# Two layers of memory attention and FFN on one core: the first tiles one by one, two pairs of heads by column tiles, other times in the planner

## The chip, the cores and the metric

The kernel runs on one core of a Trainium2 chip. The metric is the device time of one execution in microseconds (us), lower is better; before the change the median of three runs is 567.0 us (565.68 to 568.76). Engines: PE (TensorE, matmuls; PEld are its weight loads), ACT (ScalarE), DVE (VectorE), POOL (GpSimd) and SP (SyncE), which issues nearly all DMA transfers from one queue, in order.

## The reference

Two layers over x of 2048 tokens by 640 features, in bf16. Each layer is an attention with a compressive memory, then an FFN, both on a layer norm without weights, both added to x:

```python
x = x + _A_ref(_layernorm(x), A_wq, A_wk, A_wv, A_wo, A_beta)
x = x + _B_ref(_layernorm(x), B_w1, B_w2)
x = x + _A_ref(_layernorm(x), A_wq, A_wk, A_wv, A_wo, A_beta)
x = x + _B_ref(_layernorm(x), B_w1, B_w2)
```

The attention has 32 heads of 20 features and cuts the tokens into 4 segments of 512:

```python
for s in range(N):                                  # N = 4
    logits = einsum('bhqd,bhkd->bhqk', qs, ks) * scale + mask
    a_dot = einsum('bhqk,bhkd->bhqd', softmax(logits), vs)
    pq = phi(qs)                                    # x+1 above 0, exp(x) else
    a_mem = (pq @ M) / (pq @ z + 1e-6)
    outs.append(g * a_mem + (1 - g) * a_dot)        # g = sigmoid(beta)
    M, z = M + phi(ks)^T @ vs, z + sum(phi(ks))
o = concat(outs) @ wo
```

The FFN is `relu(x @ w1) @ w2` with 1728 hidden features.

## The kernel before

The kernel is a program that plans itself. Each part of the work is a Python generator (a stream) that yields operations with an assumed duration, what they wait for, and the buffers (`Slot`) that they need. `Sched.run` takes again and again the operation that can start first by its own clock, ties by the stream's priority, and so writes a fixed instruction order for every engine; semaphore waits come only from data and buffers. `late` plays a finished order again with random delays of the transfers, and the best of 32 plans, which differ in the assumed price of a mode change on PE, is emitted. Wrong assumed times make no wrong result; they make an order in which an engine stands waiting in front of work that is ready behind it.

`Sched.keep_busy` (L627 in the profile) puts dummy matmuls on PE where the order has a gap of PE over 0.3 us. `ld`, `late_loads` and `turn` hold the assumed times of loads and of DMA transposes (`lat` is the time from the last byte to the semaphore, `holds` says that the queue stays taken). All the DMA transposes, loads, spills and fills go through SP's queue.

The stages. A tile is 128 tokens, a segment four tiles, a chunk 128 of the 640 features.

- The head: `first_ln_a` normalises tiles 0 and 1 with statistics on DVE (`stats`, L651), `first_ln_b` tiles 2 and 3, tile 2 with two ACT passes that sum (L753, L757), tile 3 on DVE. `chain` (L665) raises the variance to -1/2 on POOL, `normed` (L705) writes the normalised tile, and `first_pair` transposes it on PE (L728) into one of the four `MISC` banks of PSUM and copies it to xnT (L734 on DVE, L735 on ACT). `proj_first` then projects segment 0 to q and k, in groups of five matmuls over 256 tokens each (`group`, L640 and L643; copies to `stg` at L816, L817). When both halves of a chunk's q and k are there, `first_heads` (L913) sends the first heads to `pad`. `consts` begins its POOL memsets (L580 to L594) when all four tiles are transposed. `phi_` (L956, L963, L964) makes phi of q and k, `spill` (L889) and `fill` (L934) bring the other heads through DRAM.
- Attention: groups of four heads, eight groups a segment, two groups a pair (`m`, 32 pairs in both layers). `scores` (L1103) runs row-tiled matmuls into X and Y, two slots of two PSUM banks; `exps` (L1155) takes the exponentials on ACT; `causal` (L1167) masks on POOL; `apply` multiplies by the values.
- Values have two forms. Segment 0 of layer 0, pairs 0 to 3, goes through `values_by_token` (L1197): 40 matmuls a group, tokens on the partitions, and DVE divides straight out of PSUM (L1209, L1210, L1213). All other pairs use column tiles (L1246): 16 matmuls a group, four heads beside each other, heads on the partitions. The result is copied to `av` (L1254 on DVE, L1255 on ACT), transposed by a DMA to `avt` (`turn_av`) and divided there (`divide`, L1282, L1283, L1290). There is one `av` and one `avt`.
- `combine` adds what was read from the memory, `turn_o` transposes o_sb to oT by DMA, `out_proj` multiplies by wo and adds to x (L1317), `ln_b` normalises, `ffn` and `ffn_last` (L1394) follow. PE holds one of three tiling modes (full, rows, cols), and a change of it costs time, so the planner joins a column group to the rows in front of it where it can.

DMA transposes are recorded at L671, late loads at L528 to L536.

Of the kernel before, what the change touches and what calls it, by code (L numbers as in the profile page):

```python
# [6 lines left out]
dt = mybir.dt  # L7
ACT = mybir.ActivationFunctionType
ALU = mybir.AluOpType

T = 2048
D = 640
# [148 lines left out]
STARTS = [SWITCH_NS + 0.75 * (k - 32 // 2) for k in range(32)]  # L161
# [4 lines left out]
IDLE_NS = 300.0  # L166
COLD_NS = 8000.0
# [5 lines left out]
class Sched:  # L173
# [93 lines left out]
    def run(self):  # L267
        while True:
# [22 lines left out]
            for prio, n, st, alts, op, late in heads:  # L291
# [61 lines left out]
    def late(self, seed):  # L353
# [5 lines left out]
        for e, hold, tail, waits, out, is_dma in self.log:  # L359
            m = SEM_NS + (PE_MARGIN if e == "pe" else 0.0)  # L360
            start = max([t[id(k[0]), k[1]] + m for k in waits], default=0.0)
            start = max(free[e], start)
            free[e] = start + hold
            if is_dma:
                dma_free = max(dma_free, start + 300.0) + tail[1]
                land = max(dma_free, free[e]) + tail[0] + rnd.expovariate(1.0 / LATE_NS)
                if tail[2]:
                    free[e] = max(free[e], dma_free)
# [39 lines left out]
def plan(switch, sb, sem_, psum, dram, A_x, A_wq, A_wk, A_wv, A_wo, A_beta, B_x, B_w1, B_w2, out):  # L408
# [115 lines left out]
    def late_loads():  # L524
# [27 lines left out]
        for n, (name, nbytes, fn) in enumerate(pieces):  # L552
# [7 lines left out]
            tk = yield dma("sp", sems[name], nbytes, fn, w[:1] + (w2w if n >= n2 else []) + z1, issue=400.0, lat=4500.0)  # L560
# [96 lines left out]
    def chain(t0, n, tk, sq=None):  # L657
# [7 lines left out]
        tk = yield pool(760, lambda e: e.tensor_tensor(rstd[:, sl], lnU[:, sl], mhalf[:, 0:n], ALU.pow), [tk] + h)  # L665
        return tk

    def turn(slot_sem, dst, src, waits):
# [3 lines left out]
                       issue=max(1400.0, 140.0 * n), lat=2000.0, rate=270.0, holds=True)  # L672
        return tk

    def lnorm(s, x_tks, pool_, parts=1):
# [3 lines left out]
        for p0 in range(0, 4, n):  # L679
# [11 lines left out]
            for i in range(p0, p0 + n, 2):  # L691
# [6 lines left out]
                tT = yield from turn(xn_sem[id(bx)], xt.ap[:, i * FC:(i + 2) * FC, :], bx.ap, [t0, t1] + xt.tks)  # L698
# [10 lines left out]
    def first_pair(p, tch):  # L709
        idt = yield Need("ident")  # L710
        if p == 0:
            xt = yield Acq(XNT_A)
            xt.users = []
            S.set("xts", 0, 0, tks=[xt])
        else:
            xt = yield Need("xts", 0, 0)
            xt = xt[0]
        bx = yield Acq(XN)
        done = []
        tns = []  # L720
        for k in range(2):
            tn = yield normed(2 * p + k, k, bx, tch[k])
            tns.append(tn)
        for k in range(2):
            t = 2 * p + k
            tn = tns[k]
            pb = lambda bk: bk.ap.bitcast(dt.bfloat16)
            fns = [(lambda e, bk, c=c, k=k: e.transpose(  # L728
                pb(bk)[:, c * 128:(c + 1) * 128], bx.ap[:, k * D + c * 128:k * D + c * 128 + 128], ident[:]),
                c == FC - 1) for c in range(FC)]  # L730
            bk, tT = yield pe((88.0 if p == 0 else 56.0) * FC, fns, [tn] + idt, acq=MISC)
            dst = xt.ap[:, t * FC:(t + 1) * FC, :].rearrange("p c n -> p (c n)")
            src = pb(bk)[:, 0:D]
            tc = yield evac(D, 1.5, lambda e, dst=dst, src=src: e.tensor_copy(dst, src),  # L734
                            lambda e, dst=dst, src=src: e.activation(dst, src, ACT.Copy), [tT])  # L735
            bk.release(tc)
            done.append(tc)
        bx.release(tT)
        S.set("xt", 0, 0, p, tks=done)

    def first_ln_a():
        tch = []
        for t in range(2):
            w = yield Need(("x0a", "x0b")[t])
            tk = yield from stats(t, w)
            tk = yield from chain(t, 1, [tk])
            tch.append(tk)
        yield from first_pair(0, tch)

    def first_ln_b():  # L750
        w = yield Need("x01")
        junk = hT[:, 10:13, :].rearrange("p c n -> p (c n)")[:, 0:D]
        t0 = yield act(D + 350, lambda e: e.activation(  # L753
            junk, x_sb[:, 2, :], ACT.Copy, accum_out=asum[:, 0:1]), w, psum=False)
        tm = yield dve(2, 1, lambda e: e.tensor_scalar(
            mv[:, 2, 0:1], asum[:, 0:1], 1.0 / D, None, ALU.mult), [t0])
        t1 = yield act(D + 470, lambda e: e.activation(  # L757
            junk, x_sb[:, 2, :], ACT.Square, scale=-1.0, bias=mv[:, 2, 0:1],
            accum_out=asum[:, 2:3]), [tm], psum=False)
        t3 = yield from stats(3, w)  # L760
        t1 = yield dve(1, 1, lambda e: e.tensor_scalar(
            lnU[:, 2:3], asum[:, 2:3], 1.0 / D, LN_EPS, ALU.mult, ALU.add), [t1])
        t3 = yield dve(1, 1, lambda e: e.tensor_scalar(lnU[:, 3:4], mv[:, 3, 1:2], LN_EPS, None, ALU.add), [t3])
        h = yield Need("mhalf")
        tch = yield pool(760, lambda e: e.tensor_tensor(
            rstd[:, 2:4], lnU[:, 2:4], mhalf[:, 0:2], ALU.pow), [t1, t3] + h)
        yield from first_pair(1, [tch, tch])
# [56 lines left out]

    def proj_first():
# [740 lines left out]
```

## Time and profile before

| what | value |
|---|---|
| median of three runs | 567.0 us (565.68 to 568.76) |
| the profiled execution | 565.3 us, its span 563.5 us |
| granted TensorE clock | 1.00 |
| PE, DVE, ACT, POOL busy | 99%, 75%, 72%, 35% |
| chain that ended last | PE 87%, DVE 8%, DMA 2% |

The time of an execution is the span, from the first to the last instruction, and about 1.8 us around it. Rows of a timeline give the start, the duration, the engine (SPq is SP's queue), the line, the operation, output<-input, shapes and how many of them were merged; what stands in brackets is how long the engine had been idle and what released it. Rows of the waits give who waited for what: in total, how many times, and the longest. Matmuls are pipelined: the time that one takes from the engine is read from one start to the next, not from its duration.

### The profile page before, as it was taken

To read this page: it belongs to the slowest core of one execution; us is meant where nothing else is said; L and a number is where in the kernel's file an instruction comes from. 1 tells how busy PE (TensorE), PEld (TensorE's weight loads), DVE (VectorE), ACT (ScalarE), POOL (GpSimd) and SP (SyncE) were. 2 spreads that over 40 slices of the span, in tenths; PEclk is the share of its full clock that TensorE was granted. 3 is DMA by queue.
4 is the path that set the end of the run, shared out by engine and by line. 5 is a ranking of instruction groups with operands and counts; after the bars stand their busy time and mean duration, and the time that the engine had idled before them with its cause. 6 is when DMAs were issued, how large, how long until landed. Compare 5 with 4: busy or idle time off the path is not lost.

```text
span 563.5 us, 12875 instructions
## 1 busy us (share of the span) xinstructions
PE 556.4 (99%) x5219; PEld 305.0 (54%) x5219; DVE 420.1 (75%) x1070; ACT 404.2 (72%) x512; POOL 195.1 (35%) x302
## 2 busy tenths in 40 slices
PE   8999999999999999999999999999999999999998
PEld 7664555445554454645446544555445654665655
DVE  6989789888999689878898997688747964560202
ACT  4789998987788878778986688778878678113140
POOL 4544344333344335444433443035322433110000
PEclk9999999999999999999999999999999999999999
DMA  8695988383474136542375131880326410512101
GB/s 268 120 221 138 238 218 182 74 224 56 97 171 94 44 88 159 118 95 72 92 163 115 27 66 26 193 148 20 67 80 173 109 43 20 116 45 48 47 1 47
DMA packets 130109, 60.93 MB, mean 108 GB/s; under 512 B 108930, under 2 KB 119938, under 8 KB 130050
## 3 DMA queue, kind: packets, MB, share of 16 engines
q1 hardware_dynamic: 129830, 59.85, 45.5%
q8 instruction: 41, 0.67, 0.5%
q10 hardware_dynamic: 220, 0.26, 0.2%
q14 instruction: 18, 0.15, 0.1%
HBM read 20.57 MB, written 12.85 MB: 59 GB/s over the span
## 4 chain that ended last, share of the span: by engine, by line
PE 87%; DVE 8%; DMA 2%; ACT 1%; SPq 1%; issue 0%
PE ps L643 56%; PE ps L640 11%; PE ps L1103 8%; PE ps L1246 6%; DVE stats L651 2%; PE ps L996 2%; PE ps L1197 1%; PE ps L1047 1%; DVE x_sb L1317 1%; PE ps L1394 1%; DMA avt<-av 1%; DVE xn_tok L705 1%; SPq L913 1%; DMA oT<-o_sb 1%; ACT PT L1155 1%; DVE stg L816 1%
## 5 line engine op out<-in xcount | busy, mean ns | idle before, releaser
L1155 ACT ACTIVATE PT<-ps 128x1024 bf16<-128x1024 f32 x320 | 310.0, 1022 | 70.3 <-PE ps L1103 64.6
L1167 POOL TENSOR_SCALAR_AFFINE_SELECT PT<-PT 128x512 bf16<-128x512 bf16 x256 | 166.6, 668 | 268.2 <-ACT PT L1155 267.9
L643 PE MATMUL ps<-w_r,hT 128*128 128x320 bf16 (+2 forms) x768 | 123.0, 299 | 0.0
L643 PE MATMUL ps<-xnT,w_r 128*128 128x512 bf16 x416 | 113.3, 379 | 0.0
L1317 DVE TENSOR_TENSOR x_sb<-x_sb,ps 128x320 bf16<-128x320 bf16 (+1 forms) x128 | 60.3, 479 | 66.7 <-PE ps L643 66.0
L643 PEld LDWEIGHTS ps<-w_r,hT 128*128 128x128 bf16 x768 | 72.4, 98 | 31.9 <-issue 4.4
L1425 ACT ACTIVATE hT<-ps 128x512 bf16<-128x512 f32 x55 | 32.7, 598 | 50.0 <-PE ps L643 49.7
L1103 PE MATMUL ps<-pad 20*128 20x128 bf16 (+3 forms) x1024 | 64.8, 301 | 1.6 <-ACT PT L1155 0.9
L643 PEld LDWEIGHTS ps<-xnT,w_r 128*128 128x128 bf16 x416 | 39.7, 98 | 44.0 <-issue 3.2
L651 DVE BATCH_NORM_STATS2 stats<-x_sb 128x6 f32<-128x320 bf16 x126 | 56.4, 472 | 2.1 <-DMA x_sb<-in_A_x_dram 1.8
L1254 DVE CAST av<-ps 128x512 bf16<-128x512 f32 x53 | 36.2, 684 | 14.8 <-PE ps L1246 14.7
L1103 PEld LDWEIGHTS ps<-pad 20*128 20x128 bf16 x1024 | 18.3, 92 | 52.6 <-ACT PT L1155 25.6
L643 PE MATMUL ps<-wo_r,oT 128*128 128x320 bf16 x256 | 46.1, 299 | 0.0
L1246 PE MATMUL ps<-PT,v_aug 128*32 128x256 bf16 (+5 forms) x896 | 40.7, 302 | 0.0
L1423 DVE TENSOR_SCALAR hT<-ps 128x512 bf16<-128x512 f32 x49 | 33.4, 683 | 9.1 <-PE ps L643 9.0
L640 PE MATMUL ps<-xnT,w_r 128*128 128x512 bf16 x104 | 39.6, 380 | 0.0
L643 PE MATMUL ps<-wv_r,xnT 128*128 128x320 bf16 x192 | 36.7, 300 | 0.0
L643 PE MATMUL ps<-xnT,wk_r 128*128 128x512 bf16 (+1 forms) x140 | 36.1, 349 | 0.0
L643 PE MATMUL ps<-xnT,wq_r 128*128 128x512 bf16 (+1 forms) x140 | 34.9, 349 | 0.0
L665 POOL TENSOR_TENSOR rstd<-lnU,mhalf 128x2 f32<-128x2 f32 (+2 forms) x25 | 20.8, 831 | 38.0 <-DVE lnU L661 34.4
L816 DVE CAST stg<-ps 128x512 bf16<-128x512 f32 (+1 forms) x48 | 29.5, 618 | 3.3 <-PE ps L643 3.2
L1290 DVE TENSOR_TENSOR o_sb<-avt,rden 128x320 bf16<-128x320 bf16 x56 | 30.5, 562 | 0.6
(117 smaller groups left out, 695.8 us busy)
## 6 DMA issues: line engine op xcount, KB each, us to landing
pad<-scr SPq DMA_DIRECT2D x124, 80.0 KB
scr<-stg SPq DMA_DIRECT2D x34, 256.0 KB, 2.9
out_dram<-x_sb SPq DMA_DIRECT2D x15, 160.0 KB, 1.8
w_r<-in_B_w_dram SPq DMA_DIRECT2D x10, 216.0 KB, 4.2
w_r<-in_B_w_dram SPq DMA_DIRECT2D x13, 160.0 KB, 2.8
x_sb<-in_A_x_dram SPq DMA_DIRECT2D x9, 160.0 KB, 2.8
scr<-w_r SPq DMA_DIRECT2D x5, 256.0 KB, 3.6
x_sb<-in_A_x_dram SPq DMA_DIRECT2D x3, 320.0 KB, 7.2
```

The lines of the kernel that those rows point to most:

```text
L640: bk, tk = yield pe(mm_ns(n), [(lambda e, bk, a=a, b=b: e.matmul(bk.ap[:, 0:n] if len(b.shape) == 2 else bk.ap[:, 0:n].rearrange("p (i n) ...
L643: tk = yield pe(mm_ns(n), [(lambda e, k=k, a=a, b=b, bk=bk: e.matmul(bk.ap[:, 0:n] if len(b.shape) == 2 else bk.ap[:, 0:n].rearrange("p (i ...
L651: tk = yield dve(320, 1, lambda e, c2=c2: e.bn_stats(stats6[:, t, c2, :], x_sb[:, t, c2 * 320:(c2 + 1) * 320]), xt)
L816: te = yield evac(N, 1, lambda e, sg=sg, bk=bk: e.tensor_copy(sg.ap[:, t0:t0 + N], bk.ap[:, 0:N]), lambda e, sg=sg, bk=bk: e.activation(sg ...
L1103: fns.append([(lambda e, z=z, j=j, hh=hh, N=N, o=o, sl=sl: e.matmul(ps[:, hh, o:o + N], sl.ap[32 * hh:32 * hh + DH, z, 0, 128 * j:128 * j ...
L1155: tx = yield act(1024, lambda e, dst=dst, src=src: e.activation(dst, src, ACT.Exp, scale=SCALE), sc + pw)
L1167: tm = yield pool(600.0, lambda e, reg=reg: e.affine_select(out=reg, in_=reg, pattern=[[0, 4], [1, 128]], compare_op=ALU.is_ge, fill=0.0, ...
L1246: fns.append((lambda e, bk, j=j, hh=hh, pt=pt, g=g0 + z: e.matmul(bk.ap[32 * hh:32 * hh + wide(g, hh), 128 * j:L], VAUG[vx(a, s)][:, j].re ...
L1254: te = yield evac(L, 1, lambda e, sl=sl, z=z, bk=bk: e.tensor_copy(sl.ap[:, z], bk.ap), lambda e, sl=sl, z=z, bk=bk: e.activation(sl.ap[:, ...
L1317: ta = yield dve(n, 1, lambda e: e.tensor_tensor(x_sb[:, t, c0:c0 + n], x_sb[:, t, c0:c0 + n], bk.ap[:, 0:n], ALU.add), [tk] + list(waits) ...
L1423: th = yield evac(512, 1, lambda e, dc=dc, bk=bk: e.tensor_scalar(hT[:, dc, :], bk.ap[:, :], 0.0, None, ALU.max), lambda e, dc=dc, bk=bk: ...
L1425: lambda e, dc=dc, bk=bk: e.activation(hT[:, dc, :], bk.ap[:, :], ACT.Relu), [tk] + HT.tks)
```

## The change

1. The head works by single tiles. `first_tile(t)` replaces `first_ln_a`, `first_ln_b` and `first_pair`: tiles 0 and 1 take their statistics on DVE, tiles 2 and 3 both on ACT; each tile gets its own power on POOL, its own normalising, and is transposed into X or Y instead of a MISC bank. Tiles 0 and 1 are copied to xnT by DVE. The list `TURN` writes DVE's order of the small operations out by hand. `proj_tile` projects tiles 0 and 1 separately, 128 tokens a matmul, for two chunks of k and q, into four PSUM banks that are held until tile 1 is added. Then one group of chunk 2 comes ahead of the second half of chunks 0 and 1.
2. `BY_TOKEN` is (2, 3): pairs 0 and 1 use column tiles, with `av`, the DMA transpose and `divide`; pairs 2 and 3 stay by token.
3. The planner assumes other times (loads one by one, transposes by kind, late loads 3.5 us in place of 4.5, POOL's power 0.6 in place of 0.76), lets an ACT or DVE operation count as late unless its DMAs landed 0.8 us before, adds 0.6 us to landings of DMAs that start between 8 and 106 us, charges a PE gap over 0.8 us with one more in `late`, and draws 48 plans in place of 32.

The core of the diff:

```diff
-STARTS = [SWITCH_NS + 0.75 * (k - 32 // 2) for k in range(32)]
+STARTS = [SWITCH_NS + 0.75 * (k - 48 // 2) for k in range(48)]
+SURE_NS = 800.0
+EARLY_NS = 600.0
+LOADS_NS = 106e3
+COOL_NS = 1000.0
...
+                if alts and alts[0][3] in ("act", "dve"):
+                    sure = max([self.at(t) for t in op.waits if self.P.lane(t) == "dma"], default=0.0)
+                    late = max(late, sure + SURE_NS - alts[0][1])
...
-                self.t[(id(tk[0]), tk[1])] = max(self.dma_free, end) + tail[0]
+                self.t[(id(tk[0]), tk[1])] = max(self.dma_free, end) + tail[0] + (EARLY_NS if 8e3 < start < LOADS_NS else 0.0)
...
+            if e == 'pe' and start - free[e] > 800.0 and start > 10e3:
+                start += COOL_NS
...
-        tk = yield dma(e, sem_("d_" + name), nbytes, fn, waits, lat=2200.0)
+        tk = yield dma(e, sem_("d_" + name), nbytes, fn, waits, lat={"x0a": 1950.0, "x0b": 1950.0, "x01": 1500.0, "wk0": 2900.0, "wq0": 2900.0, "wk1": 2900.0, "wq1": 2500.0, "wv": 2200.0, "x10": 3800.0, "x11": 3800.0}.get(name, 2200.0))
...
+    TURN = ["s0", "s0", "a0", "s1", "l0", "s1", "n0", "m2", "a1", "l1", "m3", "c0", "n1", "l2", "c1"]
...
+    def first_tile(t):
+        p, k = divmod(t, 2)
+        w = yield Need(("x0a", "x0b", "x01", "x01")[t])
+        if p == 0:
+            for c2 in range(2):
+                tk = yield from in_turn("s%d" % t, dve(320, 1.1, lambda e, c2=c2: e.bn_stats(
...
+        else:
+            junk = hT[:, 10 - 3 * k:13 - 3 * k, :].rearrange("p c n -> p (c n)")[:, 0:D]
+            ta = yield act(D + 350, lambda e: e.activation(
+                junk, x_sb[:, t, :], ACT.Copy, accum_out=asum[:, t:t + 1]), w, psum=False)
+            tm = yield from in_turn("m%d" % t, dve(60, 1, lambda e: e.tensor_scalar(
...
+            ta = yield act(D + 470, lambda e: e.activation(
+                junk, x_sb[:, t, :], ACT.Square, scale=-1.0, bias=mv[:, t, 0:1],
...
+        bk, tT = yield pe((88.0 if t == 0 else 56.0) * FC, fns, [tn] + idt, acq=[X, Y])
...
+        if p == 0:
+            tc = yield from in_turn("c%d" % t, dve(D, 1.5, lambda e: e.tensor_copy(dst, src), [tT], urgent=True))
+        else:
+            tc = yield evac(D, 1.5, lambda e: e.tensor_copy(dst, src),
+                            lambda e: e.activation(dst, src, ACT.Copy), [tT])
...
+    def proj_tile(t, n, c):
...
+        for k in range(FC):
+            mm = lambda e, bk, k=k: e.matmul(
+                bk.ap[:, 128 * t:128 * t + 128], w_r[:, k, c * 128:(c + 1) * 128],
+                xt.ap[:, t * FC + k, :], start=(k == 0), stop=(k == FC - 1))
...
     def proj_first():
-        order = [(c, n, h) for h in range(2) for c in range(2) for n in range(2)]
+        for t in range(2):
+            for n in range(2):
+                for c in range(2):
+                    yield from proj_tile(t, n, c)
+        order = [(2, 0, 0)] + [(c, n, 1) for c in range(2) for n in range(2)]
...
-    BY_TOKEN = ((0, 0),)
+    BY_TOKEN = (2,3)
...
-    S.add(5, first_ln_a())
-    S.add(5, first_ln_b())
+    for t in range(4):
+        S.add(1 + 0.2 * t, first_tile(t))
```

`turn` has a `lat` of its own now: 2.4 us for normalised tiles and o_sb, 1.6 for `av`, 2.0 for phi of k as before.

More of the change, by code (lines that the diff above doesn't have):

```diff
@@ L714, in first_pair @@
             S.set("xts", 0, 0, tks=[xt])
-        else:
[L716 to L767, printed above, removed]
@@ new lines, in first_tile @@
+        if k == 0:
+            bx = yield Acq(XN)
+            S.set("bx", p, tks=[bx])
+        xt = yield Need("xts", 0, 0)
+        bx = yield Need("bx", p)
+        xt, bx = xt[0], bx[0]
+        if p == 0:
+            tn = yield from in_turn("n%d" % t, normed(t, k, bx, tch))
+        else:
+            tn = yield normed(t, k, bx, tch)
+        pb = lambda bk: bk.ap[:, 0, :].bitcast(dt.bfloat16)
+        fns = [(lambda e, bk, c=c: e.transpose(
+            pb(bk)[:, c * 128:(c + 1) * 128], bx.ap[:, k * D + c * 128:k * D + c * 128 + 128], ident[:]),
+            c == FC - 1) for c in range(FC)]
@@ L770, in proj_ln @@
+        HALF[p].append((t, tT, tc))
+        S.set("xtt", t, tks=[tc])
+        if len(HALF[p]) == 2:
+            bx.release(*[x[1] for x in HALF[p]])
+            S.set("xt", 0, 0, p, tks=[x[2] for x in sorted(HALF[p])])
     def proj_ln(a, s):
@@ L1259, in apply @@
         yield from done_values(a, s, g0, tk)
-    LATER = range(len(BY_TOKEN) * G // 2, NSEG * G)
+    LATER = [m for m in range(NSEG * G) if m not in BY_TOKEN]
     def turn_av(m):
```

78 lines of the change are left out of this document (66 added, 12 removed).

## The prediction

> **What bounds the kernel now.** I read the page first, for the span and the engine that is never free.
>
> ```profile
> span 563.5 us, 12875 instructions
> PE 556.4 (99%) x5219; PEld 305.0 (54%) x5219; DVE 420.1 (75%) x1070; ACT 404.2 (72%) x512; POOL 195.1 (35%) x302
> ```
>
> PE is busy for 99% of the span. That share is an average, so I read next the busy times of the stage that the change touches, from the first exponentials to the end of segment 0's. The columns are the stretch, its length, then the busy time of PE, PEld, DVE, ACT and POOL. Below them is one line of the waits between 19 and 85 us.
>
> ```profile
> 19.50:76.00 56.50, 56.44 (x682) 32.81 (x679) 50.17 (x136) 51.94 (x70) 23.60 (x35) 1.00 0.81 191
> 42.00:56.00 14.00, 14.00 (x168) 7.03 (x169) 14.00 (x39) 12.72 (x16) 6.60 (x10) 1.00 0.56 140
> ```
>
> ```profile
> ACT PT L1155 <- PE ps L1103: 4.7, 10, 1.1
> ```
>
> Here PE is full (56.44 of 56.50 us), ACT has 4.56 us free, almost all of it waits for scores (4.7 us), and DVE has 6.33 us free, but none between 42 and 56. So a chain runs through the stage: scores on PE, exponentials on ACT, values on PE, division on DVE. Its end is in the timeline around 80 us.
>
> ```profile
> 77.35 2.71 SPq L671 DMA_TRANSPOSE phk<-phs  x1
> 78.66 0.48 DVE L1213 TENSOR_TENSOR o_sb<-ps,rden 128x320 bf16<-128x320 f32 x1
> 80.02 0.39 PE L1103 MATMUL ps<-pad 20*128 20x256 bf16 x6
> 80.10 3.16 SPq L671 DMA_TRANSPOSE oT<-o_sb  x2
> 80.34 1.40 PE L627 MATMUL ps<-ident 128*128 128x128 bf16 x22
> 82.00 0.51 PE L627 MATMUL ps<-ident 128*128 128x128 bf16 x6
> 82.44 0.73 PE L1246 MATMUL ps<-PT,v_aug 128*32 128x512 bf16 x16
> 83.10 0.70 PE L1103 MATMUL ps<-pad 20*128 20x384 bf16 x8
> 84.00 0.31 PE L640 MATMUL ps<-wo_r,oT 128*128 128x320 bf16 x1 [0.21 <-DMA oT<-o_sb]
> ```
>
> This is what the argument hangs on. L627 are dummy matmuls, put where the order has no work for PE. From 80.34 to 84.00, 3.66 us, PE does little of use: the column values (0.66) and scores, perhaps 1.3 us in all. The rest, about 2.3 us, is a hole: segment 0's output projection waits for oT. The last product of o_sb ends at 79.14, but SP is in a transpose until 80.06 and issues oT at 80.10. PE work saved before 80 us therefore only widens this hole, unless the chain itself ends earlier. After 84 us there is always a next matmul, and a microsecond of PE is a microsecond of time.
>
> **The change, part by part.**
>
> Values of pairs 0 and 1 by column tiles. In the fence: a group by token and what follows it, then groups by shape (busy, mean ns), then the transposes.
>
> ```profile
> 70.35 1.18 PE L1197 MATMUL ps<-w_r,PT 128*128 128x21 bf16 x40
> 71.38 1.02 PE L643 MATMUL ps<-hT,wk_r 128*128 128x512 bf16 x4
> ```
>
> ```profile
> L1254 DVE CAST av<-ps 128x512 bf16<-128x512 f32 x53 | 36.2, 684 | 14.8 <-PE ps L1246 14.7
> L1290 DVE TENSOR_TENSOR o_sb<-avt,rden 128x320 bf16<-128x320 bf16 x56 | 30.5, 562 | 0.6
> L1282 DVE RECIPROCAL rden<-avt 128x32 f32<-128x32 bf16 x28 | 9.6, 342 | 6.7 <-DMA avt<-av 6.7
> L1283 DVE TENSOR_TENSOR rden<-rden,omg 128x32 f32<-128x32 f32 x28 | 8.3, 296 | 0.5
> L1213 DVE TENSOR_TENSOR o_sb<-ps,rden 128x320 bf16<-128x320 f32 x8 | 3.9, 485 | 0.1
> L1210 DVE TENSOR_TENSOR rden<-rden,omg 128x16 f32<-128x16 f32 x8 | 2.2, 270 | 0.1
> L1209 DVE RECIPROCAL rden<-ps 128x16 f32<-128x16 f32 x8 | 2.0, 250 | 1.0 <-PE ps L1197 1.0
> ```
>
> ```profile
> L671 SPq DMA_TRANSPOSE avt<-av x28: 1231/1240/1911, 95.4 to 484.8; - x28
> ```
>
> By token a group holds PE 71.38-70.35 = 1.03 us; by columns 83.10-82.44 = 0.66. Four groups save 4 x 0.37 = 1.5 us of PE, if each follows scores, as at 82.44 it does not: there it comes out of full matmuls, and the change of mode is in neither number. DVE pays. A pair by token costs 2 x (250+270+485) = 2.01 us; by columns 2 x 684 + 342 + 296 + 2 x 562 = 3.13. Two pairs add 2.2 us, unless ACT takes the casts. SP's queue gets two transposes of 1.24 to 1.9 us more, and the pads, spills and weights behind them start that much later. The cover is DVE's 6.33 us and SP's idle time. For the time, the ends are 0 (the hole takes it all) and -1.5. ACT's only idle time in the stage is its wait for scores, and PE is full, so I lean to the full end: -1.0.
>
> The head, tile by tile.
>
> ```profile
> 4.62 0.74 ACT L753 ACTIVATE hT<-x_sb 128x640 bf16<-128x640 bf16 x1 [1.88 <-DMA x_sb<-in_A_x_dram]
> 6.23 0.83 ACT L757 ACTIVATE hT<-x_sb,mv 128x640 bf16<-128x640 bf16 x1 [0.78 <-DVE mv L755]
> 6.61 0.45 PE L728 MATMUL ps<-ident,xn_tok 128*128 128x128 bf16 x5 [0.35 <-DVE xn_tok L705]
> 8.24 0.49 DVE L734 COPY xnT<-ps 128x640 bf16<-128x640 bf16 x1 [0.24 <-PE ps L728]
> 8.88 0.27 PE L640 MATMUL ps<-xnT,wk_r 128*128 128x256 bf16 x1
> 11.62 0.27 PE L640 MATMUL ps<-xnT,wk_r 128*128 128x256 bf16 x1
> 12.16 0.27 PE L640 MATMUL ps<-xnT,wq_r 128*128 128x256 bf16 x1
> 12.78 1.42 DVE L956 TENSOR_SCALAR rtmp<-stg 128x512 bf16<-128x512 bf16 x1 [1.78 <-ACT stg L817]
> 13.02 1.04 POOL L586 MEMSET maskg<- 128x756 bf16 x1
> 14.12 0.41 DVE L816 CAST stg<-ps 128x256 bf16<-128x256 f32 x1
> 14.62 4.73 SPq L913 DMA_DIRECT2D pad<-stg  x6
> 19.30 0.40 PE L1103 MATMUL ps<-pad 20*128 20x512 bf16 x4 [0.62 <-DMA pad<-stg]
> ```
>
> Today projections begin at 8.88, 0.15 us after tile 1's copy (8.24+0.49). Tile 0's transposes end at 7.06. A DVE copy of 0.49 then ends at about 7.6, or 7.75 if the four small statistics ahead of it in the written order delay it, so tile 0's projections start near 7.9, 1.0 us sooner, in what is idle PE time. The same number of columns is streamed in twice as many matmuls; their extra weight loads run beside the stream, as PEld is only half busy. But tiles 2 and 3 now both take their statistics from ACT, in series: passes of 0.74 and 0.83. Tile 3's second pass cannot start before tile 2's ends and before its own mean, which stands in DVE's order behind tile 0's normalising and tile 1's aggregate. If POOL is late with tile 0's rstd, tile 2's mean, both means' passes and the copy wait with it. Now tile 2's second pass ends near 7.25 (6.23+0.83 and a read of its sum), and the second half's first matmul is at 11.62, 4.4 us later, over two tiles. With tile 3's second pass ending near 8.8 (an estimate from these durations) and one normalising and one copy fewer behind it (0.9), the second half starts near 12.3, 0.65 later. The one group of chunk 2 moved ahead of it fills 0.54 (12.16-11.62) of that. The four misc banks stay taken until tile 1 is added, so that group also waits for the first of their copies (0.41 for 256 columns, row 14.12), beside the other three groups. For PE the head is even.
>
> For the chain, the second half of chunk 0's q counts: PE finished it at 12.7, its copy stood on DVE behind L956 until 14.12, and SP sent the first pad at 14.62. In the new head the group ends near 13.4; copied at once, it leaves at 13.9 (-0.7); held up as today, at 15.3 (+0.7). I take -0.2.
>
> Transfer times and margins. The program gets no new wait; its order changes, DVE's by the written turns and all engines' by the planner. PE's wait of 0.62 for the first pad should go, as landings in the first 106 us count 0.6 us later and a PE gap is charged more when one of the 48 candidates is chosen; what is late next is the hole at 80. Ends 0 and -0.62; -0.3.
>
> Behind the head, PE's waits over the whole run are short:
>
> ```profile
> PE ps L1103 <- ACT PT L1155: 0.9, 3, 0.4
> PE ps L640 <- DVE av L1254: 0.4, 2, 0.2
> PE ps L996 <- DVE om_sb L1007: 0.2, 1, 0.2
> ```
>
> 1.5 us is all that a better order can win here. A reshuffled one can lose as much: for it no row has a price, so I take the same 1.5 upward. Half the gain: -0.75.
>
> The sum: -1.0 - 0.2 - 0.3 - 0.75 = -2.25 us. The profiled execution took 565.3 us, its span and 1.8 around it; after, 563.05. It lies 1.7 under the median of 567.0, so the forecast for the median is 567.0 - 2.25 = 564.75, say 564.8, or -0.4%. By the ends alone: -1.5-0.7-0.62-1.5 = -4.3 (562.7) and 0+0.7+0+1.5 = +2.2 (569.2).
>
> **Rivals.** Everything is cashed: PE's 1.5 us go straight into earlier scores, the hole does not grow, the order is clean. For it: PE is full until 80. Against it: ACT has only 4.7 us to win there. 562.7.
>
> Hidden anyway: the chain ends when it does today, oT lands near 84, and the hole is 1.5 us wider. For it: dummies at 80.34. Against it: ACT's waits. Only a trifle from the order is left: 566.5.
>
> Slower: two pairs more through DVE and SP. For it: DVE has 14.00 us of work in 14.00 from 42 to 56, where pair 1's division falls. From the point where no gap of DVE is left ahead of the last product of o_sb, the 2.2 us come onto the chain, and SP's transposes can push oT by a further 0.96 (80.10-79.14): +3.2, 570.2. Against it: ACT can take casts. The Trainium skill, "TensorEngine Tiling (Array Packing)", section "PSUM Bottleneck", warns of just this, that tiling speeds the matmuls and not the emptying of PSUM; the rows above agree that the copy is the added cost.
>
> Held up in the head: L956 took 1.42 us and ended at 14.20, just behind POOL's memset (14.06). These memsets start once tiles 0 to 3 are copied, so they move later with tile 3, and the copy can be caught again: +0.7 instead of -0.2, 565.7. The Trainium skill, "SBUF — State Buffer", section "SBUF: two separate sides", says of the port pair which DVE and GpSimd share that it is locked for a whole instruction and the other blocks; by that rule the lock recurs, and the trace's L956 agrees.
>
> **How the numbers follow.** A change under 0.5%, 2.8 us, can hardly be told from none here. Chances: forecast 0.42 (its own range 562.5 to 566.5; 0.16 of it beyond 0.5%), all cashed 0.22, hidden 0.10, slower 0.16, held up in the head 0.10. Faster: 0.16+0.22 = 0.38. Slower: 0.14 of the slower case and 0.01 each of hidden and held up, 0.16. The same: 0.46. The range takes in 562.7 less 1.7 for the spread of runs, and the slower case: 561.0 to 570.0.
>
> **What would show it.** Projections from about 7.9 us and a second half near 12.3; the first pad issue between 13.9 and 15.3; 160 matmuls on L1197 and 960 on L1246; 30 avt transposes; dummies still near 80 us, and oT issued about a microsecond sooner. I am wrong if oT comes later than 80.10, if DVE stands full before it, or if new PE waits beyond 1.5 us appear behind 84 us.

## The result, and the profile after

The changed kernel takes 565.12 us (median of 20 runs, 564.32 to 566.08), the kernel before in the same comparison 566.5 (median of 20, 564.97 to 568.76). The ratio is 0.9977, with a 95% interval of 0.9968 to 0.9986: a gain of about 1.4 us, or 0.2%. It is real by its interval, but below the 0.5% named in the prediction. The profiled execution took 565.11 us and its span is 563.0 us. That is 0.5 us shorter than the profiled span of before, whose execution took 565.3 us, near the lower end of before's runs. The gain is larger at the upper end of the runs than at the lower: the lowest times differ by 0.65 us, the highest by 2.7. And the time outside the span grew: it is about 2.1 us in all 20 runs of after, and 1.75 in the runs of before that were taken beside the experiments. So about 0.3 us of what the span gains is lost outside it; no trace shows why.

The page of after opens with the span and the engines; below them, from the windows, stand the stage of the first exponentials and values, and the stretch around the output projection of segment 0 (length, then busy time of PE, PEld, DVE, ACT and POOL).

```profile
span 563.0 us, 12728 instructions
PE 556.8 (99%) x5137; PEld 303.2 (54%) x5138; DVE 413.0 (73%) x1065; ACT 408.3 (73%) x519; POOL 196.8 (35%) x303
...
19.50:76.00 56.50, 56.50 (x627) 30.96 (x627) 50.43 (x137) 52.92 (x71) 24.00 (x35) 1.00 0.89 205
70.00:84.00 14.00, 13.42 (x160) 6.68 (x158) 13.81 (x40) 13.32 (x17) 6.77 (x11) 1.00 0.80 198
```

The stage is as full as before (56.50 of 56.50 us). ACT works 0.98 us more in it (52.92 against 51.94), DVE only 0.26 more; ACT's waits for scores in it fell from 4.5 to 3.2 us. The head comes next, from the timeline.

```profile
4.70 0.74 ACT L753 ACTIVATE hT<-x_sb 128x640 bf16<-128x640 bf16 x1 [1.95 <-DMA x_sb<-in_A_x_dram]
5.44 0.72 ACT L753 ACTIVATE hT<-x_sb 128x640 bf16<-128x640 bf16 x1
7.69 0.73 PE L868 MATMUL ps<-xnT,wk_r 128*128 128x128 bf16 x10 [0.17 <-DVE xnT L792]
11.02 0.27 PE L651 MATMUL ps<-xnT,wk_r 128*128 128x256 bf16 x1
11.57 0.27 PE L651 MATMUL ps<-xnT,wk_r 128*128 128x256 bf16 x1
12.73 1.63 DVE L1020 TENSOR_SCALAR rtmp<-stg 128x512 bf16<-128x512 bf16 x1 [1.57 <-ACT stg L851]
13.17 1.05 POOL L597 MEMSET maskg<- 128x756 bf16 x1
14.28 0.40 DVE L850 CAST stg<-ps 128x256 bf16<-128x256 f32 x1
14.71 4.72 SPq L977 DMA_DIRECT2D pad<-stg  x6
19.48 0.40 PE L1167 MATMUL ps<-pad 20*128 20x512 bf16 x4
```

Projections begin at 7.69 in place of 8.88. The row at 11.02 is the group of chunk 2 that was moved ahead, the row at 11.57 the start of the second half, which began at 11.62 before. The first pads leave at 14.71 (before 14.62), behind a DVE operation of 1.63 us that overlaps a POOL memset, as before. PE's wait of 0.62 us at the first scores is gone: the row at 19.48 has no bracket.

The hole around 80 us, in the timeline (L638 are the dummies):

```profile
77.09 8.66 ACT L1219 ACTIVATE PT<-ps 128x1024 bf16<-128x1024 f32 x9 [0.28 <-PE ps L1167]
77.88 3.60 SPq L682 DMA_TRANSPOSE oT<-o_sb  x2
80.98 0.34 PE L1060 MATMUL ps<-BD,w_r 128*128 128x84 bf16 x3 [0.58 <-DVE w_r L1028]
83.55 0.62 PE L638 MATMUL ps<-ident 128*128 128x128 bf16 x8
84.10 0.39 PE L1167 MATMUL ps<-pad 20*128 20x512 bf16 x2
84.66 0.33 PE L1060 MATMUL ps<-BD,w_r 128*128 128x84 bf16 x3
84.83 0.30 PE L651 MATMUL ps<-wo_r,oT 128*128 128x320 bf16 x1
```

oT is issued at 77.88, 2.2 us sooner, yet the first matmul that uses it starts at 84.83, 0.83 later than before. It is no longer oT that PE waits for. oT lands 5.4 us after its issue, near 83.3, which is 1.5 us ahead of that matmul; before, it landed 3.9 us after its issue at 80.10 and was used at once. Ahead of the matmul stand, in PE's order, the scores at 84.10 and the reading of the memory at 84.66, with dummies in front of both. The scores need the room that the exponentials free, and ACT works on these, one behind the other, from 77.09 to 85.75; in the kernel without dummies, below, the same scores wait 0.16 us for ACT. Between 76 and 88 us stand 36 dummies; before, 28.

These are PE's longest waits in the waits of the whole run (who waited for whom, total, times, longest), without the 1.6 us at the very start that both kernels have; the last three lie behind 84 us:

```profile
PE ps L1060 <- DVE w_r L1028: 0.6, 1, 0.6
PE ps L651 <- DMA oT<-o_sb: 0.5, 1, 0.5
PE ps L651 <- DVE av L1318: 0.3, 1, 0.3
PE ps L1060 <- DVE BD L1132: 0.3, 1, 0.3
```

Four waits of before in the 20 us behind the hole, 0.84 us in all, do not occur in after. The first and the last of them, from the timeline of before:

```profile
94.88 0.39 PE L1103 MATMUL ps<-pad 20*128 20x512 bf16 x2 [0.27 <-ACT PT L1155]
...
100.11 0.31 PE L640 MATMUL ps<-wv_r,xnT 128*128 128x320 bf16 x1 [0.22 <-DVE av L1254]
```

To see where the time went, I counted in both traces, at chosen times, the columns of all real matmuls that had not started yet, and turned them into microseconds by the full rate of their mode (mode changes not counted). What before still has to do, less what after has, is 2.1 us at the start (the four changed groups, with a by-token matmul of 21 columns counted as one of 64; by the prediction's price, which holds the time of whole groups, it is 1.5), 3.3 at 20 us, 1.9 at 76, 0.1 at 85, 1.8 at 106 and 1.7 at 430, 0.65 at 460 and 0.5 at the end. So after is ahead through the head, loses the lead in the hole, regains it in the 20 us behind it, and loses about 1.1 between 430 and 460.

### The profile page after: what moved, and what is told of

It is laid out like the page before. It is cut to its first block, busy times and chain, and to the rows that moved or that the text cites. A ratio compares the mean times of both kernels' runs of the same rounds, so it can differ in the third digit from the quotient of the medians.

```text
span 563.0 us, 12728 instructions
## 1 busy us (share of the span) xinstructions
PE 556.8 (99%) x5137; PEld 303.2 (54%) x5138; DVE 413.0 (73%) x1065; ACT 408.3 (73%) x519; POOL 196.8 (35%) x303
## 4 chain that ended last, share of the span: by engine, by line
PE 88%; DVE 8%; ACT 2%; issue 1%; DMA 1%; POOL 0%; POOLq 0%
PE ps L654 56%; PE ps L651 11%; PE ps L1167 8%; PE ps L1310 6%; PE ps L1060 2%; ACT PT L1219 1%; PE ps L1111 1%; DVE stg L850 1%; DMA oT<-o_sb 1%; PE ps L634 1%; DVE o_sb L1354 1%; PE ps L1458 1%; DVE stats L662 1%; DVE rtmp L1020 1%; DVE av L1318 0%
## 5 line engine op out<-in xcount | busy, mean ns | idle before, releaser
L1231 POOL TENSOR_SCALAR_AFFINE_SELECT PT<-PT 128x512 bf16<-128x512 bf16 x256 | 168.3, 675 | 268.4 <-ACT PT L1219 268.2
L1489 ACT ACTIVATE hT<-ps 128x512 bf16<-128x512 f32 x59 | 35.3, 598 | 53.0 <-PE ps L654 52.7
L1167 PE MATMUL ps<-pad 20*128 20x512 bf16 (+3 forms) x1024 | 65.6, 301 | 0.0
L662 DVE BATCH_NORM_STATS2 stats<-x_sb 128x6 f32<-128x320 bf16 x120 | 53.5, 472 | 0.3
L1310 PE MATMUL ps<-PT,v_aug 128*32 128x128 bf16 (+4 forms) x896 | 40.7, 302 | 0.0
L1487 DVE TENSOR_SCALAR hT<-ps 128x512 bf16<-128x512 f32 x45 | 30.7, 683 | 8.1 <-PE ps L654 8.0
L654 PE MATMUL ps<-xnT,wq_r 128*128 128x512 bf16 (+1 forms) x132 | 33.3, 354 | 0.0
L1354 DVE TENSOR_TENSOR o_sb<-avt,rden 128x320 bf16<-128x320 bf16 x60 | 32.5, 562 | 0.5
L850 DVE CAST stg<-ps 128x512 bf16<-128x512 f32 (+1 forms) x44 | 27.8, 633 | 4.5 <-PE ps L654 4.5
L1310 PEld LDWEIGHTS ps<-PT,v_aug 128*32 128x32 bf16 (+1 forms) x896 | 18.9, 96 | 21.9 <-issue 7.2
```

Of the source, the lines that this page charges most:

```text
L654: tk = yield pe(mm_ns(n), [(lambda e, k=k, a=a, b=b, bk=bk: e.matmul(bk.ap[:, 0:n] if len(b.shape) == 2 else bk.ap[:, 0:n].rearrange("p (i ...
L662: tk = yield dve(320, 1, lambda e, c2=c2: e.bn_stats(stats6[:, t, c2, :], x_sb[:, t, c2 * 320:(c2 + 1) * 320]), xt)
L850: te = yield evac(N, 1, lambda e, sg=sg, bk=bk: e.tensor_copy(sg.ap[:, t0:t0 + N], bk.ap[:, 0:N]), lambda e, sg=sg, bk=bk: e.activation(sg ...
L1167: fns.append([(lambda e, z=z, j=j, hh=hh, N=N, o=o, sl=sl: e.matmul(ps[:, hh, o:o + N], sl.ap[32 * hh:32 * hh + DH, z, 0, 128 * j:128 * j ...
L1231: tm = yield pool(600.0, lambda e, reg=reg: e.affine_select(out=reg, in_=reg, pattern=[[0, 4], [1, 128]], compare_op=ALU.is_ge, fill=0.0, ...
L1310: fns.append((lambda e, bk, j=j, hh=hh, pt=pt, g=g0 + z: e.matmul(bk.ap[32 * hh:32 * hh + wide(g, hh), 128 * j:L], VAUG[vx(a, s)][:, j].re ...
```

## Experiments

The first three undo one part each. Every such edit makes the planner draw a new order for all engines.

**Values of pairs 0 and 1 by token again.**

```diff
-    BY_TOKEN = (2,3)
+    BY_TOKEN = (0, 1, 2, 3)
```

> The changed kernel, with pairs 0 to 3 all by token again (BY_TOKEN holds 0, 1, 2 and 3). Theory A, the hole: what PE saves before 78 us is spent on dummies ahead of segment 0's output projection, so taking the 1.5 us of savings away leaves the time where the changed kernel is, 565.1 us or a ratio of 0.998 to the kernel before, within 0.5 us; the dummies around 78 to 85 us shrink instead. Rival B, PE is the bound throughout: PE has 1.5 us more to do and the time rises by it, to a ratio of about 1.000.

Measured: 568.2 us, ratio to before 1.0031 (1.001 to 1.0052). No theory had expected a kernel slower than before. Its waits, in an execution of 569.37 us, show why it decides little:

```profile
PE ps L1310 <- DVE v_aug L931: 2.0, 1, 2.0
PE ps L1111 <- DMA phk<-phs: 1.3, 3, 0.7
```

The one of 2.0 us lies at about 184 us, 100 us behind the edited stage. All waits of PE in its timeline, the brackets added up, come to 8.1 us, against 3.6 in after and 4.7 in before.

**The head of before.**

```diff
-    TURN = ["s0", "s0", "a0", "s1", "l0", "s1", "n0", "m2", ...
-    def first_tile(t):
...
-    def proj_tile(t, n, c):
...
+    def first_ln_a():
...
+    def first_ln_b():
...
+    def first_pair(p, tch):
...
```

> The changed kernel with the head of the kernel before (pairs of tiles, tile 3's statistics on DVE, no written order of DVE). The head was even for PE in the forecast and worth 0.2 us for the chain; the trace of the changed kernel has the first pad issue at 14.71 us, against 14.62, so the head should be worth nothing by itself: a ratio of 0.998 again. If the earlier projections (7.69 us against 8.88) are carried to the end, the time rises by about 1 us, to 0.9995.

Measured: 568.09 us, 1.0036 (1.0019 to 1.0052); PE waits 6.7 us in all, 1.2 of it for one transpose of phi of k.

**The planner's times and margins of before.**

```diff
-STARTS = [SWITCH_NS + 0.75 * (k - 48 // 2) for k in range(48)]
-EARLY_NS = 600.0
-COOL_NS = 1000.0
+STARTS = [SWITCH_NS + 0.75 * (k - 32 // 2) for k in range(32)]
+EARLY_NS = 0.0
+COOL_NS = 0.0
...
-                if alts and alts[0][3] in ("act", "dve"):
-                    sure = max([self.at(t) for t in op.waits if self.P.lane(t) == "dma"], default=0.0)
-                    late = max(late, sure + SURE_NS - alts[0][1])
...
-            tk = yield dma("sp", sems[name], nbytes, fn, w[:1] + (w2w if n >= n2 else []) + z1, issue=400.0, lat=3500.0)
+            tk = yield dma("sp", sems[name], nbytes, fn, w[:1] + (w2w if n >= n2 else []) + z1, issue=400.0, lat=4500.0)
...
```

> The changed kernel with the planner's old times, no margins and 32 plans: the new head and the new values alone. If the gain comes from the order, as the remaining work at 106 us (1.8 us less) against 90 us (none less) suggests, the ratio goes back to 1.000. If it comes from head and values, it stays at 0.998.

Measured: 571.75 us, 1.0095 (1.007 to 1.012); PE waits 8.1 us.

The three undone parts lose 3.1, 3.0 and 6.6 us against after (568.2, 568.09 and 571.75 less 565.12). Together that is nine times the gain of the whole change, so these are not the prices of the parts: each kernel also carries the luck of its new order. How large that luck is can be measured without touching any part.

**The second and third cheapest candidate order, of after and of before.** The edit, for the second (for the third, index 2):

```diff
-        S = min(plans, key=lambda p: sum(p.late(n) for n in range(4)))
+        costs = [sum(p.late(n) for n in range(4)) for p in plans]
+        S = plans[costs.index(sorted(set(costs))[1])]
```

> The changed kernel, but the second cheapest of the 48 candidate orders in place of the cheapest. If the three runs with one part undone were slower mainly because each drew a new order (PE's waits add up to 7 to 10 us in them, against 4 in the kernels before and after), this one is slower as well, by 1 to 4 us (ratio 1.000 to 1.005), with more waits of PE. If the parts themselves made the difference, it stays at 0.998.

> The same with the third cheapest order. Luck of the order: 1 to 4 us slower than the changed kernel. Parts: 0.998.

> The kernel before, but the second cheapest of its 32 candidate orders. Luck of the order: slower than the kernel before by 1 to 4 us, ratio 1.002 to 1.007. If the planner's choice hardly matters on the chip, 1.000 within 0.001.

> The kernel before with the third cheapest of its 32 orders. So far the kernel before has 1.000 and 1.0025 for its two cheapest orders, the changed kernel 0.998, 1.0025 and 1.008. If the order is luck on the chip in both, this one lies anywhere from 1.002 to 1.010; if the old planner's orders are the more alike, it stays below 1.003.

| candidate by the planner's cost | after | before |
|---|---|---|
| cheapest (the kernels themselves) | 565.12 us, 0.9977 | 566.5 us, 1 |
| second | 567.67 us, 1.0025 (1.0014 to 1.0037) | 567.76 us, 1.0025 (1.0012 to 1.0038) |
| third | 570.77 us, 1.0082 (1.006 to 1.0104) | 572.14 us, 1.0099 (1.0071 to 1.0127) |

One row of the waits of after's third candidate and one of before's third:

```profile
PE ps L651 <- DVE v_aug L931: 2.1, 1, 2.1
...
PE ps L1047 <- DMA phk<-phs: 3.1, 2, 2.6
```

The three candidates that the planner rates best differ by up to 5.7 us, as the theory of luck expected (the third of after is beyond its 4 us). Single waits of 2 us or more, such as these, are a large part of it: PE's waits add up to 7.4 and 9.8 us in the two third candidates. Many waits are also what the kernels with a part undone have. In the three ranks after lies below before by 1.4, 0.1 and 1.4 us, but in the second the ratios are equal and in the third the intervals overlap: only the first pair shows a gain clear of noise.

In before's third candidate a wait costs more than its length. These are two stretches around the end of its wait of 2.6 us, which lies at about 61 us; the column after POOL is the granted clock:

```profile
60.00:64.00 4.00, 2.85 (x20) 1.81 (x20) 0.86 (x2) 0.60 (x1) 0.00 (x0) 0.54 0.55 125
64.00:68.00 4.00, 4.00 (x21) 1.88 (x15) 2.05 (x5) 2.31 (x4) 1.22 (x2) 0.61 0.55 158
```

The clock falls to 0.50 during the wait and stays there for 6.8 us. Of this candidate's six runs, the two with a mean clock of 1.00 take 569.92 and 570.04 us, the four with a lower one 571.94 to 574.47.

What follows: in this kernel a part can be priced only with the order held fixed. The next experiments do that.

**PE a microsecond later in the head, in the order of after.** 18 dummies stand ahead of tile 0's first projection; the computation is unchanged.

```diff
-                FIRST[c, n], tk = yield pe(mm_ns(128), [(mm, False)], w + x, acq=MISC)
+                idle = lambda e, bk: e.matmul(bk.ap[:, 0:128], ident[:], ident[:], start=True, stop=True)
+                fns = [(idle, False)] * (18 if (c, n) == (0, 0) else 0) + [(mm, False)]
+                FIRST[c, n], tk = yield pe(mm_ns(128), fns, w + x, acq=MISC)
```

> The changed kernel in its own order, with 18 dummy matmuls (18 x 0.056 = 1.0 us) ahead of tile 0's first projection: PE starts its useful work where the kernel before did. Theory A, the hole at 78 to 85 us takes what PE saves ahead of it: the time stays at 565.1, ratio 0.998. Rival B, PE carries it through: +1.0 us, ratio 0.9995. In between, the 36 dummies in the hole are kept, so only PE's real waits there (0.64 us in the trace) can give way: then about +0.4.

Measured: 567.05 us, 1.0011 (0.9994 to 1.0028), span 565.0, which is 2.0 more than after. Since the order is that of after, the same instruction can be followed through both traces. First this kernel's timeline, then two rows of after for comparison:

```profile
7.61 1.18 PE L872 MATMUL ps<-ident 128*128 128x128 bf16 x18 [0.20 <-DVE xnT L792]
8.63 0.72 PE L868 MATMUL ps<-xnT,wk_r 128*128 128x128 bf16 x10
78.76 2.10 SPq L682 DMA_TRANSPOSE oT<-o_sb  x1
85.71 0.30 PE L651 MATMUL ps<-wo_r,oT 128*128 128x320 bf16 x1
358.72 3.56 SPq L1000 DMA_DIRECT2D pad<-scr  x6
363.64 0.39 PE L1169 MATMUL ps<-pad 20*128 20x512 bf16 x4 [0.75 <-DMA pad<-scr]
```

```profile
357.81 2.41 SPq L998 DMA_DIRECT2D pad<-scr  x6
361.94 0.40 PE L1167 MATMUL ps<-pad 20*128 20x512 bf16 x4
```

The first projection is 0.94 us later than in after (8.63 against 7.69), oT's issue 0.88 (78.76 against 77.88), the first output matmul 0.88 (85.71 against 84.83). From 28 to 361 us every matmul starts 0.87 to 0.89 us later than in after. With its dummies the hole swallows nothing: the chain that fills it hangs on PE's own scores 60 us earlier and moves with them. At 358.72 a group of six fills, 0.91 us late, occupies SP's queue for 3.56 us in place of 2.41, and PE, which had not waited there, waits 0.75. From then on the delay is 1.70 (363.64 against 361.94). At 416 us a wait for DVE adds 0.25, and then the delay stays at 1.95 to the end. One of the six fills holds the queue for 1.49 us; why, I did not find out. Lateness alone does not do it: in the kernel without dummies, below, the same six start 4.13 us later than in after and take 2.41 again.

**The values of pairs 0 and 1 as dear as by token, in the order of after.** Five dummies stand ahead of each of the four column groups.

```diff
+            if m < 2:
+                idle = lambda e, bk: e.matmul(bk.ap[:, 0:128], ident[:], ident[:], start=True, stop=True)
+                fns = [(idle, False)] * 5 + fns
             bk, tk = yield pe(545.0, fns, mk + vt, acq=MISC, mode="cols")
```

> The same 1.6 us ahead of pairs 0 and 1, with all dummies kept. Theory A: the dummies are now in the way, and only PE's real waits in the hole (0.64 us) give way, so +1.0 us, ratio 0.9995. Rival B: +1.6 us and more, ratio 1.0005 or above. Against the run with fewer dummies this tells what the dummies of the hole are worth when PE comes late.

Measured: 568.39 us, 1.0037 (1.0023 to 1.005), span 565.7.

```profile
79.35 2.14 SPq L682 DMA_TRANSPOSE oT<-o_sb  x1
86.30 0.30 PE L651 MATMUL ps<-wo_r,oT 128*128 128x320 bf16 x1
364.27 0.40 PE L1167 MATMUL ps<-pad 20*128 20x512 bf16 x4 [0.77 <-DMA pad<-scr]
```

oT leaves 1.47 us later than in after, the first output matmul starts 1.47 later, and at 364.27 the same wait for fills makes it 2.33. At the end it is 2.7 us of span, and 3.3 between the medians. What PE saves in these groups is therefore worth its full price and, in this order, more.

**The same with three quarters of the dummies between 76 and 90 us left out.** The edit is the one above and this:

```diff
+        if 76e3 < start < 90e3:
+            n = n // 4 + 1
```

> The changed kernel in its own order, with 5 dummies ahead of each of the four value groups of pairs 0 and 1 (4 x (0.28 + a change of mode of 0.12) = 1.6 us: as dear as by token) and 23 fewer dummies (1.3 us) between 78 and 85 us. Theory A, the saved PE time only became dummies: the first matmul on oT stays near 84.8 and the time at 565.1, ratio 0.998 within 0.001. Rival B, dearer values delay the scores and so the chain: oT and the end come up to 1.6 us later, ratio 1.0005, with PE idle in the hole as long as the missing dummies.

Measured: 568.38 us, 1.0035 (1.0018 to 1.0052), span 566.9. It says nothing on the values, because the granted clock fell in the hole to 0.50 (84 to 88 us). The next kernel shows the same.

**No dummies after 20 us, in the order of after.**

```diff
-        if gap < IDLE_NS or self.idle_fn is None:
+        if gap < IDLE_NS or self.idle_fn is None or start > 20e3:
```

> The changed kernel with the same order, less the dummy matmuls that the planner puts after 20 us (52 of them, 44 between 78 and 85 us). Theory A1, the dummies themselves hold the place: 36 x 0.056 = 2.0 us less between 78 and 85 us, and the first matmul on oT starts when oT has landed, near 83.3 in place of 84.83: about 1 us is won, 564. Theory A2, the hole is a wait for data: the dummies are replaced by waits, and the time stays at 565.1 within 0.4 us.

Measured: 568.37 us, 1.0033 (1.0018 to 1.0048), 3.2 us more than after. Of the 52 dummies 36 lie between 78 and 85 us. In the windows the column after POOL is the granted clock; two rows of this kernel, then one of after.

```profile
80.00:84.00 4.00, 3.19 (x34) 1.19 (x34) 3.57 (x10) 3.62 (x5) 2.04 (x3) 0.77 1.14 204
84.00:88.00 4.00, 3.69 (x23) 1.46 (x21) 2.99 (x10) 2.74 (x4) 2.01 (x3) 0.50 1.32 155
```

```profile
84.00:88.00 4.00, 4.00 (x41) 2.52 (x39) 2.88 (x9) 3.96 (x5) 1.86 (x3) 1.00 0.96 189
```

The profiled execution is the slowest of the twelve, 569.29 us, and its span is 4.2 us longer than that of after. Followed through both traces, the same matmul comes 0.22 us later in this kernel at 76 us, at the same time at 81.48 (without its dummies the hole does take up a little), and 2.27 us later at 88; a wait of 1.3 us for a transpose of phi of k at 222 us is the largest piece of the rest. The hole does not close without dummies: its matmuls start when their data are there, in both kernels (L1060 waits for w_r at the same place). Nor does oT end it: it lands 4.4 us after its issue at 78.10, near 82.5, and its first matmul starts at 85.44. But the clock falls to 0.50 and the real matmuls behind the hole, 23 between 84 and 88 us, run at half speed. The dummies are not waste; they are what keeps the clock at 1.00 through a stretch where PE has gaps.

**The two POOL memsets out of the way, in the order of after for all other engines.** The memsets of ones, into `v_aug` and w_r, go to the start, the one of `maskg` behind the copy of chunk 0's q.

```diff
-        xt0 = yield Need("xt", 0, 0, 0)
-        xt1 = yield Need("xt", 0, 0, 1)
+        tv = []
...
-            v_aug[:].rearrange("p b j h e -> p (b j h) e")[:, :, DH:DH + 1], 1.0), xt0 + xt1)
+            v_aug[:].rearrange("p b j h e -> p (b j h) e")[:, :, DH:DH + 1], 1.0), tv)
...
-        t3 = yield pool(700, lambda e: e.memset(maskg[:], 1.0))
+        t3 = yield pool(700, lambda e: e.memset(maskg[:], 1.0), (yield Need("stg", 0, 0, 0, 1)))
```

> The changed kernel with POOL's two memsets of ones (1.80 and 0.99 us) moved to the start, ahead of tile 0's power, and the mask's memset behind the copy of chunk 0's q. All other instructions and the order of PE, ACT, DVE and SP are the same. Theory A, the memsets hold DVE up: the rtmp of 1.63 us at 12.73 takes 0.3, chunk 0's q is copied near 13.1 in place of 14.28, SP sends the first pad near 13.5 in place of 14.71, and PE's wait of 0.3 us at 14.3 goes. The time falls by no more than that, 0.3 us to a ratio of 0.997, since PE's order has fixed work ahead of the first scores. Rival B, DVE was waiting for something else: the rtmp stays at 1.6 us. Rival C, the chain from the first pad sets the time: about 1 us less, 0.996.

Measured: 564.48 us, 0.9968 (0.9957 to 0.998), span 562.6. It is the fastest kernel of this study, though its interval overlaps that of after. Its timeline:

```profile
12.67 0.29 DVE L1020 TENSOR_SCALAR rtmp<-stg 128x512 bf16<-128x512 bf16 x1 [1.57 <-ACT stg L851]
12.88 0.42 DVE L850 CAST stg<-ps 128x256 bf16<-128x256 f32 x1
13.33 4.72 SPq L977 DMA_DIRECT2D pad<-stg  x6
19.09 0.39 PE L1167 MATMUL ps<-pad 20*128 20x512 bf16 x4
```

The DVE operation takes 0.29 us in place of 1.63: its time in after was a wait for POOL's memsets. The pads leave 1.38 us sooner, but the first scores, which stand behind projections in PE's order, start only 0.39 sooner (19.09 against 19.48), and 0.4 is what the span gains. The medians differ by 0.64, because the time outside the span is 1.8 us in this kernel and 2.1 in after.

## Why the prediction was right or wrong, by its own steps

The time was forecast as 564.8 and came out as 565.12, a gain of 1.4 us where the sum had 2.25. The direction holds; several terms do not, and the chain's has the wrong sign. That the two times lie 0.3 us apart is in part luck: before itself came out 0.5 lower than the 567.0 of the forecast, and the errors below, of 0.3 to 1.1 us each, go both ways.

- **The hole widens by what PE saves, unless the chain ends earlier.** Wrong in its first half. With the order of after held, PE time ahead of 80 us passes through the hole in full (0.94 becomes 0.88, and the 1.47 of the values stays 1.47). I had weighed PE's time and the chain's as two things; the chain's exponentials wait for PE's scores, so they are one. The ends 0 and -1.5 should have been -1.5 alone. The order of before was not tested in this way. And what ends the hole has changed: in before it is oT, as the prediction says, in after the scores and the memory reads that stand ahead of oT's matmul.
- **Values, -1.0.** The step was right, and so was the lean to the full end. The counts named came as well: 160 matmuls by token, 960 by columns, 30 transposes of `av`. One of the four groups in the timeline of after, with the full matmul behind it:

```profile
43.95 0.73 PE L1310 MATMUL ps<-PT,w_r 128*32 128x512 bf16 x16
44.62 0.39 PE L654 MATMUL ps<-hT,wk_r 128*128 128x512 bf16 x1
```

  That is 0.67 us from one start to the next, as the price taken from before said (0.66); the other three measure 0.66, 0.66 and 0.67. DVE's price was also near: in the lines of the stage the casts to `av` and the divisions by columns take 6.1 us and what is left by token 3.0, where by token alone took 7.2, so 1.9 for the 2.2 forecast. Yet DVE's sum in the stage rose by 0.26 only, mostly because its operations between SBUF buffers became shorter. The products of phi, first before and then after (busy, mean ns):

```profile
L964 DVE TENSOR_TENSOR phs<-phs,rtmp 128x512 bf16<-128x512 bf16 x11 | 5.4, 493 | 0.3 <-ACT phs L963 0.2
```

```profile
L1028 DVE TENSOR_TENSOR phs<-phs,rtmp 128x512 bf16<-128x512 bf16 x10 | 4.1, 413 | 0.9 <-ACT phs L1027 0.9
```

  The same shape takes 413 ns in place of 493. I had not expected that, and why it is so was not tested. The last product of o_sb ends at 77.85 and oT is issued at 77.88, so SP's two transposes more cost the chain nothing. So the rival "slower" fell. The Trainium skill, "TensorEngine Tiling (Array Packing)", section "PSUM Bottleneck", says that the copy out of PSUM may become the bottleneck; here DVE's work behind the matmuls rose by 1.9 us and did not become the bound.
- **The head, even.** The mis-sized term of the sum. Tile 0's projections came 1.2 us sooner (1.0 forecast), but the second half did not move to 12.3: it starts at 11.57, with the moved group of chunk 2 (0.55, 11.02 to 11.57) already done. PE is thus 0.6 ahead, not even. The working had tile 3's second ACT pass end near 8.8; both first passes ran at 4.70 and 5.44, so the second passes followed each other at 6.39 and 7.21 and ended about 8.1. I had tile 3's mean wait too long in DVE's order.
- **The chain to the first pads, -0.2.** The issue came at 14.71, inside the stated 13.9 to 15.3, but at +0.1 against before. The mechanism of the rival "held up in the head" is what happened: the DVE operation took 1.63 us beside the memsets. With them moved it takes 0.29, which shows the cause; the delay had cost 0.4 us of the span. The rival's price of 0.9 (-0.2 to +0.7) was too high, since projections cover most of the delay. The Trainium skill, "SBUF — State Buffer", section "SBUF: two separate sides", describes an exclusive lock of the port pair that DVE and GpSimd share; the two runs agree with it, though neither shows the lock itself.
- **Order: the first pad's wait, -0.3, and the later waits, -0.75.** The wait of 0.62 went altogether, so the first term was too small. Behind 84 us three waits (0.5, 0.3 and 0.3, 1.1 us) stand in place of 1.5: -0.4, half of what was forecast. No new waits beyond 1.5 us appeared there. Against it stands a loss that the sum did not have: a hole that is longer by eight dummies, 0.5 us at the 0.057 us of each (18 of them in 1.02 us). The dummies mainly mark it, and oT does not end it, though its two transposes took 4.4 and 5.4 us from issue to landing (3.5 and 3.9 before).
- **The balance.** Values and head alone give 2.1 us, the two order terms 1.0, the longer hole takes 0.5 back: -2.6. The measured medians give -1.4, of which the time outside the span has taken 0.3; the profiled spans, with an execution near the lower end of before's runs, give -0.5. The count of remaining matmuls puts 1.1 us of what is missing between 430 and 460 us, where the order of after is worse than that of before; one row of it is a wait of 0.34 for `av` at 443.29, the rest was not traced.
- **What was not in the prediction at all:** the luck of the drawn order. "For it no row has a price" was right for the trace of before, and the 1.5 us taken as its upper end was too small: the three best-rated orders lie up to 5.7 us apart. That after draws an order with no more waits than before's (3.6 and 4.7 us) is a condition of the result that the prediction did not state. A share of the gain for each of the three parts of the change cannot be given from undoing them, and stays open. With the order held, taking the values' saving back costs 2.7 us of span and the head's lead of 1 us 2.0; how much of the planner's new times is in the gain was not separated from the draw.
- **Hidden anyway** fell with the first point. **All cashed** came true for the head and the values, but its time (562.7) was not reached.

## What to carry to other kernels

Where a planner draws the order, undo a part with the order held fixed (dummies as dear as the saving, or one engine's instructions moved), and run the next candidates of the ranking before believing that a few tenths of a per cent belong to a part. A gap of the busiest engine in front of a chain is no cushion if the chain itself began on that engine: follow the chain back before crediting a saving at nothing. Before a delay on DVE is laid to its own work, look whether POOL writes at the same time.

## What the hardware showed

The granted clock fell although PE was never idle for long: in before's third candidate during a wait of 2.6 us, and in the kernel without dummies behind shorter waits. There PE was busy for 3.19 of the 4 us from 80 on, at a mean clock of 0.77, and in the next 4 us the clock was 0.50. With dummies it stayed at 1.00. The longest waits ahead of the fall, in the timeline of the kernel without dummies:

```profile
80.22 0.39 PE L1167 MATMUL ps<-pad 20*128 20x512 bf16 x2 [0.53 <-ACT PT L1219]
81.20 0.34 PE L1060 MATMUL ps<-BD,w_r 128*128 128x84 bf16 x3 [0.59 <-DVE w_r L1028]
```

A wait of 2.1 us, in after's third candidate, left the clock at 1.00 in the profiled execution. The Trainium skill, "TensorE: Matmul & The Clock Gate", section "HAM oscillation — how this bites in real kernels", gives as its rule no idle gaps above about 3.4 us; here the longest gap was 0.59 us in one kernel and 2.6 us in the other. Another section of that page of the Trainium skill, "A second HAM failure mode: psum-queue depth-cycling", speaks of frequent short idling, which is closer to these rows.

POOL's memsets stretched a DVE operation from 0.29 to 1.63 us. And the same six fills took 2.41 us of SP's queue in one run, 3.56 when they started 0.91 us later, 3.78 when they started 1.43 us later, and 2.41 again when they started 4.13 us later. First the run with 3.78, then the one that was latest:

```profile
359.24 3.78 SPq L998 DMA_DIRECT2D pad<-scr  x6
...
361.94 2.41 SPq L998 DMA_DIRECT2D pad<-scr  x6
```

In a full order a small shift can thus cost as much again further on: 0.94 us in the head became 2.0 at the end.
